# Local attention and two mixture layers on one core: where the softmax of batches 0 and 1 is normalised

## The chip, the cores and the metric

The kernel runs on one core of a Trainium2 chip. The metric is the device time of one execution in microseconds (us): a median of 918.62 us over 3 runs, from 918.5 to 919.01. One further execution was profiled and took 924.32 us, of which 922.5 us are the span from its first to its last instruction. That is 5.70 us above the median, so differences worked out on the profile are applied to the median afterwards.

## The reference, cut to what matters

Attention comes first: 4 batches, 8 heads, 512 local and 32 global positions, head size 64. Local queries see a window of 32 positions to either side and the 32 global keys. Two feed-forward stages follow.

```python
def sm(s):
    s = s - np.max(s, axis=-1, keepdims=True)
    e = np.exp(s)
    return e / (np.sum(e, axis=-1, keepdims=True) + 1e-09)
...
s_l = np.concatenate([s_lg, s_ll], axis=-1)
a_l = sm(s_l)
out_l = np.matmul(a_l, np.concatenate([v_g, v_l], axis=2))
...
h = x @ w_in
g = np.maximum(h, 0.0) + alpha * np.minimum(h, 0.0)
return (g @ w_out)
```

The division by the row sum is linear: it can be done on the probabilities `P` before the product with `V`, or on the product afterwards, row by row. The second feed-forward stage routes every token to one of 8 experts; its choice of expert needs all tokens.

## The kernel before, in words

**Tiling of the attention.** `units` are 16 pairs of heads: units 0 to 3 are batch 0, units 4 to 7 batch 1, and so on. A unit is done in two steps, j = 0 and 1, of 256 query positions each, and a step has two blocks of 128 queries for each of its two heads. For each step the functions in `attention()` run in this order, each for a step later than the one before:

- `scores` (L355): TensorE multiplies queries with 224 keys (L369) into two PSUM banks `s`. VectorE adds the mask and finds the maximum (L375, four instructions), ScalarE takes the exponential and the row sum `sm` (L377, four).
- `norm` (L380): VectorE adds 1e-9 to four columns of sums (L383), takes the reciprocal (L384), and multiplies the four 128 x 224 blocks of `pr` by it (L388).
- `ptrans` (L390): TensorE turns the probabilities (L397), ScalarE copies them to SBUF (L399).
- `pv` (L401): TensorE multiplies with the values (L408, eight products, written in pairs to partitions 0-63 and 64-127, so the output has head dimensions on partitions and queries along the columns). ScalarE copies the result to `x` (L409).

Each pair of units also has a global part: `gscores` (L420 to L426), `gnorm` (L430 to L432), `gtrans` (L439 to L446) and `gpv` (L457), whose result VectorE copies to `x` (L460).

**The first stage.** While `alone[0]` is true, only attention and the decoding of weights run. It goes on until batch 0 is complete. PSUM has 2 + 2 banks for `s`, 2 for `t`, and 2 with the tag `y`, which `o`, `gs`, `gt` and `go` share (`bank`, L317).

**The second stage.** Attention of batches 1 to 3 is then traced in turn with the first half of the first feed-forward layer: `gemm` (L174) works on chunks of 272 tokens, two chunks to a batch, with matmuls at L166 and L199. Its first matmul needs the split of chunk 0 (`splitx`, a copy on ScalarE and a subtraction on VectorE, both L67/L68), and so all of batch 0's columns up to 272. Four PSUM banks with the tag `a` serve the attention here.

**Decoding.** The weights come as 64-bit floats, read as pairs of integers. `decode` (L72) takes an absolute value on ScalarE (L77) and four passes on VectorE (L78, L80, L81, L82); `split` then copies on ScalarE (L67) and subtracts on GpSimd or VectorE (L68). There are 16 parts of 128 x 512 for the first half of the layer. The second half's 16 parts are decoded after the attention, in the memory that it leaves.

**What sets the order.** Up to the second half of that layer the order on each engine is not the order of the text: a planner in the tile framework goes over the traced instructions with its own estimates of time, and places what is ready by its estimate, earlier text first. Each engine then runs its list strictly in order. From the routing on, TensorE's order is written out by hand. Waits between engines are put in by the framework from the tiles that instructions read and write.

The functions that the change touches, and those that call them:

Of the kernel before, what the change touches and what calls it, by code (L numbers as in the profile page):

```python
# [9 lines left out]
F32 = mybir.dt.float32  # L10
# [5 lines left out]
OP = mybir.AluOpType  # L16
# [9 lines left out]
def tile_attention_moe_moe(ctx: ExitStack, tc: tile.TileContext, qkw, vw,  # L26
                           w_in, w_out, alpha, w_gate, w1, w2, out):
    nc = tc.nc
    V, A, P, T = nc.vector, nc.scalar, nc.gpsimd, nc.tensor
    B, H, S, D, SG = BHSDG  # L30
# [27 lines left out]
    ident = cp.tile([128, 128], F32, name="ident")  # L58
# [244 lines left out]
    with ExitStack() as at:  # L303
# [3 lines left out]
        tp = at.enter_context(tc.tile_pool(name="tp", bufs=2, side="right"))  # L307
# [9 lines left out]
        def bank(shape, name):  # L317
            pool, tag = pY, "y"
            if not alone[0]:
                pool, tag = pA[0], "a"  # L320
            elif name == "s":
                pool, tag = ((pS, "s"), (pS, "s"), (pH, "h1"), (pH, "h1"))[turn[0] % 4]
                turn[0] += 1
            elif name == "t":
                pool, tag = pX, "x"
            return pool.tile(shape, F32, name=name, tag=tag)

        units = [(b, hp) for b in range(B) for hp in range(H // 2)]
        NU = len(units)
        U = [dict() for _ in units]  # L330
        G = [dict() for _ in range(NU // 2)]
        KO = S + NB * KW

        def load(u):
            d = U[u]
            qk = ld.tile([128, KO + 2 * SG], F32, name="qk")
            cut_ = S + 2 * KW if u == 0 else 0
            if cut_:
                nc.sync.dma_start(out=qk[:, :cut_], in_=qkw[u, :, :cut_])
            nc.sync.dma_start(out=qk[:, cut_:], in_=qkw[u, :, cut_:])  # L340
            d["q"] = qk[:, :S]
            d["k"] = qk[:, S:KO].rearrange("p (i w) -> p i w", w=KW)
            d["g"] = qk[:, KO:]

        def load_v(u):
            d = U[u]
            vv = ld.tile([128, 2, NB, 2 * D], F32, name="vv", bufs=4)
            nc.sync.dma_start(out=vv.rearrange("p a i d -> p (a i d)"), in_=vw[u])
            d["va"], d["vb"] = vv[:, 0], vv[:96, 1]

        def heads(u):
            for h in range(2):
                yield h, slice(h * D, (h + 1) * D)

        def scores(u, j):  # L355
            d = U[u]
            if j == 0:
# [22 lines left out]
        def norm(u, j):  # L380
            d = U[u]
            sm = d["sm"][:, :, 2 * j:2 * j + 2]
            V.tensor_scalar(sm, sm, 1e-9, None, op0=OP.add)  # L383
            V.reciprocal(sm, sm)  # L384
            for ii in range(2):
                i = 2 * j + ii
                for h in range(2):
                    V.tensor_scalar(d["pr"][:, h, i], d["pr"][:, h, i], d["sm"][:, h, i:i + 1], None, op0=OP.mult)  # L388

        def ptrans(u, j, half):  # L390
            d = U[u]
            n = 96 if half else 128
            t = bank([n, 2, 2, 128], "t")
            for ii in range(2):
                for h in range(2):
                    p = d["pr"][:, h, 2 * j + ii]
                    T.transpose(t[:, ii, h], p[:, 128:KW] if half else p[:, 0:128], ident)  # L397
            d["t", j, half] = tp.tile([n, 2, 2, 128], F32, name="pt", tag="bt" if half else "at")
            A.copy(d["t", j, half], t)  # L399

        def pv(u, j):  # L401
            d = U[u]
            o = bank([128, 2, 128], "o")
            for ii in range(2):
                i = 2 * j + ii
                for half, v in enumerate(("va", "vb")):
                    for h, c in heads(u):
                        T.matmul(o[c, ii], d[v][:, i, c], d["t", j, half][:, ii, h], start=half == 0, stop=half == 1)  # L408
            A.copy(d["x"][:, SG + 256 * j:SG + 256 * j + 256], o.rearrange("p i t -> p (i t)"))  # L409

        def gscores(p, part):
            d = G[p]
# [59 lines left out]
        def attention():  # L472
# [7 lines left out]

            for n in range(2 * NU + 2):
                u, j = divmod(n, 2)
                if u < NU:
                    if j == 0 and u + 2 < NU:
                        load(u + 2)
                        load_v(u + 2)
                    scores(u, j)
                    yield 1.0
                if 1 <= n <= 2 * NU:
                    a_ = divmod(n - 1, 2)  # L490
# [6 lines left out]
                if n >= 2:  # L497
# [3 lines left out]
                    if v % 2 and j2:  # L501
                        gout(v // 2)
                        yield 0.1
                if u < NU and u % 2 == 0 and j:
                    p = u // 2
# [24 lines left out]
        while done[0] < UPB - 1:  # L530
            next(att)
            n += 1
            if n >= 6 and n % 6 == 0 and len(parts) > KD:
                f, i = parts.pop(0)
# [10 lines left out]
        c = 0  # L545
        g = None
        going = True
        while going:
# [6 lines left out]
            if spent["a"] <= spent["g"] * ratio or g is None:  # L555
                x = next(att, None)
# [4 lines left out]
            else:  # L561
                x = next(g, None)
# [3 lines left out]
                else:  # L566
                    spent["g"] += x
                    if parts:
                        f, i = parts.pop(0)
# [5 lines left out]
    with tc.tile_pool(name="dc2", bufs=1, side="right") as dc, tc.tile_pool(name="pW", bufs=2, space=PSUM) as pW:  # L575
# [3 lines left out]
        while c < NCH:  # L579
# [4 lines left out]
            while next(g, None) is not None:  # L584
                n += 1
                if n % 3 == 0 and parts:
                    f, i = parts.pop(0)
# [12 lines left out]
    with ExitStack() as mo:  # L600
# [44 lines left out]
        late = rc_.tile([128, 128], BF, name="late")  # L645
# [39 lines left out]
        for i, n in enumerate(TH + [1]):  # L685
            t = spot(n).bitcast(I32) if i else rc_.tile([128, n], I32, name="jt0")
# [571 lines left out]
```

## Time and profile before

| | |
|---|---|
| median of 3 runs | 918.62 us |
| profiled execution | 924.32 us, span 922.5 us |
| TensorE matmul busy | 854.1 us (93%) |
| VectorE busy | 561.1 us (61%) |
| ScalarE busy | 405.2 us (44%) |
| GpSimd busy | 402.1 us (44%) |
| mean granted TensorE clock | 0.966 of full speed |

PE is TensorE's matmuls, PEld its weight loads, DVE VectorE, ACT ScalarE, POOL GpSimd, SP the queue that issues most transfers. Times are from the span's start. A busy share over the span mixes stages with different limits, so each stage is read by itself. An f32 matmul is carried out as two recorded instructions, so the eight products of one `pv` appear as 16. Matmuls overlap, so a group's length contains the latency of its last one; what a group costs its engine is read from its start to the start of the next.

### The profile page before, as it was taken

What the parts mean: (1) busy time and instruction counts of PE and PEld (TensorE: products, weight loads), DVE (VectorE), ACT (ScalarE), POOL (GpSimd) and SP (SyncE); (2) the same over time, 40 slices, a digit from 0 to 9 for tenths busy, and PEclk for the clock granted to TensorE, in tenths of its full rate; (3) what the DMA queues carried; (4) which work ended last, traced back from release to release, by engine and by line L of the source; (5) the groups of instructions that cost most, each with busy time, mean ns of one, the idle gap of its engine ahead of it and who ended that gap; (6) DMA issues with size and microseconds to landing.
All of it is one profiled execution on the core that took longest, in us unless ns stands there. A gap on an engine that the chain in (4) does not pass through costs nothing.

```text
span 922.5 us, 18674 instructions
## 1 busy us (share of the span) xinstructions
PE 854.1 (93%) x7142; PEld 781.4 (85%) x7142; DVE 561.1 (61%) x1815; ACT 405.2 (44%) x945; POOL 402.1 (44%) x335
## 2 busy tenths in 40 slices
PE   6869999999998799999999897999699998899996
PEld 4648898888888799999998897999498998799995
DVE  6999665556549963266567767778266766631120
ACT  5866655455534542234332423331334534444431
POOL 2224211111115642176566515232467777777721
PEclk8988999999999999999999998999799999999998
DMA  8574323422136412032210224332445555455510
GB/s 305 178 251 159 123 74 115 118 72 88 37 129 178 146 49 73 23 100 83 65 49 1 74 72 157 98 100 87 125 141 162 162 161 174 151 164 181 168 40 35
DMA packets 50273, 107.66 MB, mean 117 GB/s; under 512 B 6728, under 2 KB 23112, under 8 KB 50184
## 3 DMA queue, kind: packets, MB, share of 16 engines
q1 hardware_dynamic: 47288, 97.56, 33.8%
q0 software_dynamic: 2896, 8.92, 2.7%
q8 instruction: 56, 0.92, 0.4%
q14 instruction: 33, 0.27, 0.1%
HBM read 88.63 MB, written 17.83 MB: 115 GB/s over the span
## 4 chain that ended last, share of the span: by engine, by line
PE 29%; DMA 10%; POOL 8%; issue 6%; DVE 3%; ACT 3%; POOLq 0%; SPq 0%; ACTq 0%
PE h L1103 10%; PE h L166 9%; DMA raw<-in_moe_w_dram 9%; POOL m L68 6%; PE h L979 2%; PE lp L238 2%; ACT m L67 2%; PE h L995 1%; POOL xg L930 1%; DVE gr L68 1%; PE yt L227 1%; PE y L199 1%; PE pc L819 1%; POOL out_dram L1029 0%; DMA x2d<-yr 0%
## 5 line engine op out<-in xcount | busy, mean ns | idle before, releaser
L68 POOL TENSOR_TENSOR m<-raw,m 128x1024 fp32r<-128x1024 f32 x64 | 152.6, 2390 | 58.3 <-ACT m L67 57.8
L166 PE MATMUL h<-xh,win 128*128 128x272 f32 x768 | 168.9, 300 | 7.5 <-ACT xh L67 3.7
L166 PEld LDWEIGHTS h<-xh,win 128*128 128x128 f32 x768 | 129.1, 192 | 15.4 <-DVE g L185 4.5
L68 POOL TENSOR_TENSOR glo<-g,ghi 128x272 fp32r<-128x272 f32 x64 | 57.6, 902 | 192.7 <-ACT ghi L67 190.6
L1103 PE MATMUL h<-gr,wout 128*128 128x272 f32 x768 | 115.1, 302 | 0.3 <-DVE gr L68 0.3
L166 PE MATMUL h<-xl,win 128*128 128x272 f32 x384 | 113.1, 295 | 1.7 <-DVE xl L68 1.7
L199 PE MATMUL y<-ghi,wout 128*128 128x272 f32 x512 | 111.8, 298 | 3.1 <-ACT ghi L67 3.0
L979 PE MATMUL h<-xsh,m 128*128 128x272 f32 x512 | 109.5, 303 | 5.2 <-ACT xsh L67 5.2
L171 DVE TENSOR_SCALAR nm<-h,al 128x272 f32<-128x272 f32 x128 | 63.4, 496 | 82.8 <-PE h L166 82.1
L1103 PEld LDWEIGHTS h<-gr,wout 128*128 128x128 f32 x768 | 103.0, 195 | 7.6 <-issue 6.6
L995 PE MATMUL h<-hh,m 128*128 128x272 f32 x512 | 103.4, 294 | 0.0
L67 ACT CAST m<-raw 128x1024 fp32r<-128x1024 f32 x64 | 66.8, 1047 | 79.8 <-DMA raw<-in_moe_w_dram 79.6
L979 PEld LDWEIGHTS h<-xsh,m 128*128 128x128 f32 x512 | 85.0, 195 | 6.5 <-ACT xsh L67 6.2
L199 PEld LDWEIGHTS y<-ghi,wout 128*128 128x128 f32 x512 | 84.0, 189 | 7.3 <-ACT ghi L67 3.9
L995 PEld LDWEIGHTS h<-hh,m 128*128 128x128 f32 x512 | 81.3, 189 | 0.9 <-issue 0.5
L199 PE MATMUL y<-glo,wout 128*128 128x272 f32 x256 | 75.3, 298 | 3.0 <-POOL glo L68 3.0
L979 PE MATMUL h<-xsl,m 128*128 128x272 f32 x256 | 76.8, 300 | 0.0
L166 PEld LDWEIGHTS h<-xl,win 128*128 128x128 f32 x384 | 74.2, 193 | 2.7 <-DVE xl L68 2.4
L995 PE MATMUL h<-hl,m 128*128 128x272 f32 x256 | 75.6, 295 | 0.1
L377 ACT ACTIVATE pr<-sc,mx 128x224 f32<-128x224 f32 x128 | 60.5, 475 | 25.4 <-DVE mx L375 25.3
L68 POOL TENSOR_TENSOR l<-gb,h 128x272 fp32r<-128x272 f32 x62 | 54.5, 893 | 22.9 <-ACT h L67 20.7
L375 DVE CUSTOM_DVE_ANT_0 sc<-s,mask 128x224 f32<-128x224 f32 x128 | 43.3, 383 | 31.4 <-PE s L369 31.4
(233 smaller groups left out, 1725.9 us busy)
## 6 DMA issues: line engine op xcount, KB each, us to landing
raw<-in_moe_w_dram SPq DMA_DIRECT2D x64, 512.0 KB, 3.6
qk<-in_qk_dram SPq DMA_DIRECT2D x15, 736.0 KB, 4.2
vv<-in_v_dram SPq DMA_DIRECT2D x16, 512.0 KB, 5.2
raw<-in_moe_w_in_dram SPq DMA_DIRECT2D x16, 512.0 KB, 5.5
raw<-in_moe_w_out_dram SPq DMA_DIRECT2D x16, 512.0 KB, 3.9
xs<-xb SPq DMA_DIRECT2D x16, 272.0 KB, 5.0
xpart<-xd SPq DMA_DIRECT2D x32, 136.0 KB, 1.8
xb<-xs SPq DMA_DIRECT2D x8, 544.0 KB, 4.3
```

What stands on the lines that cost most here:

```text
L67: A.copy(hi, src)
L68: (lo_eng or V).tensor_tensor(lo, src, hi.bitcast(F32), op=OP.subtract)
L166: T.matmul(ps, wi[:, w, k, fs], x[:, k], start=i == 0, stop=i == 3 * KD - 1)
L171: V.tensor_scalar(nm, ps, 0.0, al[:, hf * KH + f:hf * KH + f + 1], op0=OP.min, op1=OP.mult)
L199: T.matmul(ps, wo[:, w, f, ds_], x[:, f], start=i == 0, stop=i == 3 * KH - 1)
L227: T.transpose(t[:, k * 128:(k + 1) * 128], tail["x"][:, k] if q == 2 else xo[:, k, a:b], ident)
L238: T.matmul(lp, w, x, start=first and i == 0, stop=last and i == 1)
L375: V.tensor_tensor_reduce(out=sc, in0=s[h][:, ii], in1=m, scale=-D ** -0.5, scalar=BIG, op0=OP.add, op1=OP.min, accum_out=d["mx"][:, h, i:i ...
L377: A.activation(out=d["pr"][:, h, i], in_=sc, func=AF.Exp, bias=d["mx"][:, h, i:i + 1], scale=-1.0, accum_out=d["sm"][:, h, i:i + 1])
L979: T.matmul(ps, d["w1"][:, w, kk, fs], x[:, kk], start=i == 0, stop=i == 3 * KD - 1)
L995: T.matmul(ps, d["w2"][:, w, f, ms], x[:, f], start=i == 0, stop=i == 3 * K3 - 1)
L1103: T.matmul(ps[j], wo[:, w, f, ds_], x, start=f == 0 and a == 0, stop=f == KH - 1 and a == 2)
```

## The change

In batches 0 and 1 `norm` stops after the reciprocal: `pr` keeps the exponentials. In `pv` the PSUM tile doubles to two halves. TensorE first writes the reciprocals into the second half: the weights are one column of `sm`, repeated 64 times, the moving operand is the identity, so all 64 output partitions hold the row of 128 reciprocals. ScalarE copies that half to a new SBUF tile `rs`. The products with the values go to the first half as before, and VectorE multiplies the two into `x`, where ScalarE had copied. Batches 2 and 3 and the global rows are as before.

```diff
+        NBO = 2
...
             V.reciprocal(sm, sm)
+            if units[u][0] < NBO:
+                return
             for ii in range(2):
...
-            o = bank([128, 2, 128], "o")
+            late = units[u][0] < NBO
+            ot = bank([128, 2, 2, 128] if late else [128, 1, 2, 128], "o")
+            o = ot[:, 0]
+            if late:
+                for ii in range(2):
+                    for h, c in heads(u):
+                        T.matmul(ot[c, 1, ii], d["sm"][:, h, 2 * j + ii:2 * j + ii + 1].to_broadcast([128, D]), ident, start=True, stop=True)
+                rs = tp.tile([128, 2, 128], F32, name="rs")
+                A.copy(rs, ot[:, 1])
...
-            A.copy(d["x"][:, SG + 256 * j:SG + 256 * j + 256], o.rearrange("p i t -> p (i t)"))
+            x = d["x"][:, SG + 256 * j:SG + 256 * j + 256].rearrange("p (i t) -> p i t", i=2)
+            if late:
+                V.tensor_tensor(x, o, rs, op=OP.mult)
+            else:
+                A.copy(x, o)
```

## Rows read from the trace of the kernel before

**Rows 1.** The page's second part: busy tenths of each engine and TensorE's granted clock in 40 slices of 23 us.

```profile
PE   6869999999998799999999897999699998899996
...
DVE  6999665556549963266567767778266766631120
ACT  5866655455534542234332423331334534444431
...
PEclk8988999999999999999999998999799999999998
```

**Rows 2.** Busy time of each engine by stretch (the view by windows): stretch, its length, then PE, PEld, DVE, ACT and POOL busy with the number of instructions, the granted clock, the share of the DMA engines and GB/s.

```profile
6.00:16.00 10.00, 6.94 (x43) 4.23 (x40) 8.11 (x43) 5.75 (x21) 0.00 (x0) 1.00 1.02 400
16.00:40.00 24.00, 23.39 (x192) 16.76 (x192) 23.46 (x92) 22.21 (x72) 4.30 (x4) 0.79 0.58 174
40.00:52.00 12.00, 8.40 (x63) 5.97 (x63) 12.00 (x47) 10.09 (x30) 3.14 (x3) 0.79 0.98 333
52.00:66.00 14.00, 8.02 (x101) 6.25 (x100) 13.66 (x22) 8.16 (x15) 5.26 (x5) 0.94 0.60 172
66.00:76.00 10.00, 8.22 (x49) 6.79 (x49) 9.90 (x26) 6.55 (x18) 3.28 (x3) 0.66 0.73 254
76.00:92.00 16.00, 15.62 (x110) 13.05 (x109) 16.00 (x42) 8.77 (x23) 7.46 (x7) 1.00 0.40 129
92.00:140.00 48.00, 48.00 (x481) 42.88 (x481) 29.91 (x117) 28.17 (x86) 10.12 (x11) 1.00 0.31 99
140.00:266.00 126.00, 126.00 (x1197) 110.23 (x1193) 70.13 (x273) 67.16 (x202) 15.19 (x18) 1.00 0.26 81
266.00:322.00 56.00, 47.42 (x357) 44.59 (x356) 51.70 (x83) 26.64 (x52) 31.41 (x27) 1.00 0.57 178
```

**Rows 3.** The timeline at the end of the first stage, all engines: start, length, engine, line, operation, and in brackets the idle time before it with what ended it.

```profile
57.29 1.36 PE L457 MATMUL go<-gt,vv 128*64 128x32 f32 x40 [0.32 <-DVE gt L440]
...
58.66 1.73 DVE L81 SCALAR_TENSOR_TENSOR mag<-raw,mag 128x512 int32<-128x512 int32 x1
...
61.95 1.74 DVE L81 SCALAR_TENSOR_TENSOR mag<-raw,mag 128x512 int32<-128x512 int32 x1
63.73 0.69 DVE L82 SCALAR_TENSOR_TENSOR mag<-raw,mag 128x512 int32<-128x512 int32 x1
64.33 0.22 DVE L460 COPY xb<-go 128x64 f32<-128x64 f32 x1
...
64.98 1.09 ACT L67 CAST xh<-xb 128x1088 fp32r<-128x1088 f32 x1
...
66.12 0.52 PE L166 MATMUL h<-xh,win 128*128 128x272 f32 x2 [3.75 <-ACT xh L67]
```

**Rows 4.** VectorE's costliest groups from 0 to 66 us (the view by lines): count, busy, mean of one in ns, idle time before.

```profile
L375 DVE CUSTOM_DVE_ANT_0 sc<-s,mask 128x224 f32<-128x224 f32 x40 | 13.8, 379 | 6.3 <-PE s L369 6.3
L388 DVE TENSOR_SCALAR pr<-pr,sm 128x224 f32<-128x224 f32 x40 | 13.7, 400 | 0.0
L81 DVE SCALAR_TENSOR_TENSOR mag<-raw,mag 128x512 int32<-128x512 int32 x11 | 10.6, 962 | 0.2
```

**Rows 5.** What TensorE waited for from 0 to 66 us (the view of waits): total, times, longest.

```profile
PE o L408 <- DVE gmx L422: 3.2, 2, 2.4
PE s L369 <- DVE mx L375: 3.1, 1, 3.1
PE t L397 <- ACT pt L399: 1.0, 2, 0.6
PE gt L445 <- DVE gsc L432: 0.8, 1, 0.8
PE o L408 <- ACT xb L409: 0.7, 1, 0.7
...
PE go L457 <- DVE gt L440: 0.3, 1, 0.3
```

**Rows 6.** TensorE's timeline around one `pv` of the second stage, and ScalarE's copy of another.

```profile
112.21 0.41 PE L199 MATMUL y<-ghi,wout 128*128 128x272 f32 x2
112.56 1.10 PE L408 MATMUL o<-pt,vv 128*64 128x128 f32 x16
113.59 0.40 PE L199 MATMUL y<-glo,wout 128*128 128x272 f32 x1
...
115.60 0.29 PE L199 MATMUL y<-glo,wout 128*128 128x272 f32 x1
115.73 0.41 PE L199 MATMUL y<-ghi,wout 128*128 128x272 f32 x2
...
104.26 1.08 PE L408 MATMUL o<-pt,vv 128*64 128x128 f32 x16
105.39 0.37 ACT L409 COPY xb<-o 128x256 f32<-128x256 f32 x1 [1.95 <-PE o L408]
```

**Rows 7.** TensorE's `pv` instructions from 0 to 66 us (by lines), and those from 66 to 140 us with duration min/median/max in ns (the view of one line).

```profile
L408 PE MATMUL o<-pt,vv 128*64 128x128 f32 (+1 forms) x128 | 11.3, 322 | 4.4 <-DVE gmx L422 3.2 <-ACT xb L409 0.7 <-ACT gt L446 0.6
...
L408 PE MATMUL o<-pt,vv x128: 269/272/325, 75.0 to 137.5; 128*64 128x128 f32 x64, 96*64 96x128 f32 x64
```

**Rows 8.** Durations: a VectorE instruction with one PSUM and one SBUF operand (66 to 140 us), ScalarE's eight copies of `o` (0 to 66 us), and all multiplications of `pr` (min/median/max in ns).

```profile
L185 DVE SCALAR_TENSOR_TENSOR g<-h,nm 128x272 f32<-128x272 f32 x14 | 6.1, 435 | 0.7
...
L409 ACT COPY xb<-o 128x256 f32<-128x256 f32 x8 | 2.9, 365 | 0.0
...
L388 DVE TENSOR_SCALAR pr<-pr,sm x128: 319/331/1404, 9.3 to 254.7; 128x224 f32<-128x224 f32 x128
```

**Rows 9.** By windows, as rows 2, around TensorE's early change of clock.

```profile
12.00:16.00 4.00, 0.94 (x9) 0.59 (x6) 3.61 (x19) 1.94 (x7) 0.00 (x0) 1.00 1.02 407
16.00:20.00 4.00, 3.39 (x16) 2.10 (x15) 3.46 (x13) 3.35 (x10) 0.00 (x0) 0.53 0.85 179
20.00:24.00 4.00, 4.00 (x26) 2.98 (x24) 4.00 (x16) 3.69 (x13) 1.45 (x1) 0.50 0.92 300
24.00:28.00 4.00, 4.00 (x28) 2.55 (x26) 4.00 (x17) 4.00 (x16) 0.00 (x0) 0.69 0.46 177
28.00:32.00 4.00, 4.00 (x32) 2.97 (x28) 4.00 (x18) 4.00 (x11) 1.31 (x1) 1.00 0.38 125
```

**Rows 10.** VectorE's waits for TensorE's `gpv` from 92 to 266 us.

```profile
DVE xb L460 <- PE go L457: 5.0, 3, 3.7
```

## The prediction, on record before the changed kernel ran

> **What bounds the kernel now.** I read the busy tenths by slice first. TensorE is full from about 70 us to the end of the attention and has holes before; VectorE is full from the second slice to the fourth [rows 1]. So the attention lies in two stages with different limits, and the change touches both: by TensorE's `pv` instructions, 128 before 66 us and 128 from 75.0 to 137.5 us, 16 to a step, batch 0's eight steps lie in the first stage and batch 1's eight in the second [rows 7].
>
> The view by windows says which engine is short. From 16 to 66 us VectorE is busy 49.1 of 50 us, while ScalarE has 9.5 and TensorE 10.2 us to spare. From 66 to 92 VectorE is still full, but TensorE is busy 23.8 of 26, and from 92 to 266 us it is busy without a break, with VectorE at 57% [rows 2]. From 66 us on, then, TensorE sets the pace, and what VectorE does less of there buys nothing.
>
> The timeline at the border shows how the first stage ends: `gpv` ends at 58.65, yet VectorE copies it at 64.33, because decoding of weights stands in front in its list; the split of the first chunk and the first matmul of the feed-forward layer at 66.12 follow directly [rows 3]. VectorE's list is the chain that ends the stage.
>
> After the attention nothing changes. Decoding the second half of the weights begins when the attention gives its memory back and keeps VectorE busy 51.7 of 56 us [rows 2], so that stage starts earlier or later with the attention's end, and I carry the difference to the end of the kernel one to one.
>
> **The change part by part.** *Removed in the first stage.* All 40 multiplications of `pr` that the first stage holds, ten steps of units 0 to 4, which all fall under the change, stand in front of the 64.33 copy; together they keep VectorE 13.7 us [rows 4]. One takes 319 to 1404 ns [rows 8]; the group's total has the stretched ones in it.
>
> *Added there on VectorE.* Eight multiplications of 128 x 256 with one operand in PSUM. The nearest row is 435 ns for 272 columns [rows 8]; I take 0.43 us, so 3.4 us. VectorE's list gets 13.7 - 3.4 = 10.3 us shorter.
>
> *ScalarE.* One copy of 256 columns from PSUM goes (365 ns) and one of the same size comes: nothing, by count [rows 8]. The copy moves ahead of the products, so it can wait for TensorE while exponentials are queued behind it; I cost that with the rival on handoffs.
>
> *Added on TensorE.* Four f32 products per step, with 128 columns moving and 64 weight columns in pairs, half of what `pv` does. `pv` takes from 112.56 to 113.59, 1.03 us, among the feed-forward matmuls [rows 6], so half is 0.515 us. From below, nothing excludes that they fill a hole: 0 in the first stage. From above: where they stand alone, a change of kind is paid twice more. Feed-forward matmuls start 0.13 us apart (115.60, 115.73), so the second of the pair at 112.21 started at 112.34 and the next was due at 112.47; `pv` came 0.1 us late [rows 6]. That makes 0.61 us at most.
> The Trainium skill, "TensorEngine Tiling (Array Packing)", Key Properties under Tiling Modes, says that changing the tiling mode drains the engine, and the new products differ in mode from the feed-forward matmuls. That is a price for every separate block; the trace has it at about 0.1 us, and the sum by the rule would be that upper end.
>
> *What the first stage gains.* With VectorE 10.3 us shorter, its copy could stand at 54.0. TensorE is next. Its waits for VectorE from 5 to 66 us are 3.1 + 3.2 + 0.8 + 0.3 = 7.4 us [rows 5]. If all went, and the eight new blocks came in at 0.515 us, twice as much for two of them between 16 and 27 us, where the granted clock is at its lower level [rows 9] (8 x 0.515 + 2 x 0.515 = 5.2 us at most; the last one isn't needed by chunk 0, so 4.6), `gpv` would end at 58.65 - 7.4 + 4.6 = 55.9. So the matmul at 66.12 could come at most 8.5 us earlier. The lower end is 0: the planner can put more decoding in front, as it does now. Not every wait for VectorE will go, since decoding moves into the holes; I take two thirds, 5.7 us.
>
> *What the second stage loses.* Batch 1's eight blocks on a full engine: 8 x 0.515 = 4.1 to 8 x 0.61 = 4.9 us, taken as 4.5. The norms that go there were beside TensorE: no gain. From below: TensorE's holes between 66 and 92 us are 2.2 us [rows 2], and blocks that fall into them all would leave 1.9; less than nothing is excluded, since the products are added to an engine that is full from 92 us on.
>
> *The sum.* 5.7 - 4.5 = 1.2 us gained: 923.1 for the profiled execution, 917.4 for the median. Two large terms nearly cancel, so the sign is not safe. About 0.2% (1.84 us) is what a measurement of this kernel can tell from no change.
>
> **The rivals.** *The handoff inside one bank.* The reciprocals and the output share one PSUM tile. If the framework holds the products back until ScalarE has read `rs`, TensorE goes to ScalarE and back in every step. Priced by rows: the last product's own 0.27 us [rows 7], then ScalarE's copy, which today starts within 0.05 us of the products' end and takes 0.37 [rows 6], and about 0.1 back: 0.8 us if nothing else is placed between. Eight times that in the first stage is 6.4 us on the engine that I found to be next; half of it, because scores and transposes of other steps can stand between, is 3.2. Then the first stage gains 5.7 - 3.2 = 2.5 and the sum is +2.0: 920.6. It decides on the slower side once more than 1.2 us of the 6.4 are not covered. For it: TensorE already waits 0.7 us for such a copy to free a bank, and 3.2 us for the shared `y` banks, which are held longer now [rows 5]. Against it: the planner knows the wait and has other work for TensorE from 16 to 40 us.
> The Trainium skill, "PSUM — Partial Sum Buffer", section on PSUM bank collisions, says that two engines on the same bank and quadrant at once are an error and that software has to order them. By that rule the wait is real and the question is only what covers it; no run here shows it yet.
>
> *The end of the first stage stays where decoding puts it.* VectorE's freed time is filled with more parts of the weights, which stand before the 64.33 copy again. A part is four passes; L81 alone took 1.73 us twice there [rows 3], so two more parts eat half of the 10.3 us or more. A multiplication that waits for TensorE can hold the list too: one wait for `gpv` was 3.7 us [rows 10]. The gain falls to 2 us and the sum is +2.5: 921.1. For it: that is what the rows show today. Against it: those parts are then missing later, but TensorE is full there, so they bring nothing back.
>
> *The clock stays up.* After 3.1 us idle TensorE's granted clock falls at 16 us to its lower level of 1.2 GHz and is back by 28 [rows 5, 9]. That idle time ends with VectorE's L375, behind four multiplications which go. Shorter, it might leave the clock at 2.4 GHz; the 11 us of nearly full work until 27 would take half, and about 3 us of it could reach the end of the stage, where ScalarE, with 9.5 us to spare [rows 2], sets a limit of its own. The sum is -4.2: 914.4. For it: the engine before was at the higher level up to the gap. Against it: ScalarE waits for transfers in the same place.
>
> *The change does not do what it says* in one sense: that norms vanish from VectorE but the stage was held by TensorE's own work all along. From 16 to 40 us TensorE is busy 23.4 of 24 [rows 2]. Then the blocks come on top in both stages, 4.6 + 4.5 us less a few waits of the 7.4: about +4, 922.6.
>
> **How the numbers follow.** The two terms nearly cancel as worked out (from +0.4 to -2.9 us): 0.44, of which 0.20 lie beyond -1.84 and 0.24 within 0.2%. Clock stays up, or VectorE's relief reaches further: 0.20, all faster. Handoff: 0.16, of which 0.03 within 0.2%. The end stays with decoding: 0.12, of which 0.01 within. TensorE's own work: 0.08, slower. That is faster 0.40, same 0.28, slower 0.32. The forecast is that of the first case, 917.4, whose own range is 915.7 to 919.0. The range of 8 in 10 takes in -5 us at one end and +4 at the other: 913.6 to 922.4.
>
> **What would show it.** Right: VectorE's L388 falls from 128 to 64 instructions; the first feed-forward matmul comes at 59 to 62 us instead of 66.12; from there to the end of the attention the stretch is 4 to 5 us longer than 200; from 266 us on lengths are the same. The handoff would show as waits of TensorE's `o` for ScalarE's `rs`, the clock as a level near 1.0 from 16 to 28 us, decoding as a late L460 with `gpv` long done. I'd be wrong if TensorE's blocks in the second stage cost clearly more or less than 0.5 to 0.6 us, or if the stage after the attention doesn't move along with its start.

## The result, and the profile after

The changed kernel took 928.07 us (median of 4 runs, 926.8 to 929.41), the kernel before 918.82 beside it (918.5 to 919.74). These two medians are 9.25 us apart; the ratio on record is 1.0083, 95% interval 1.0053 to 1.0112: slower by 0.8%. In the later series, with 9 to 25 executions each, the kernel before has medians of 920.22 to 921.25. The forecast was 917.4, its range 913.6 to 922.4; the time lies outside. The profiled execution took 928.45 us with a span of 926.7.

Three points of time tell where it went. The first feed-forward matmul came at 71.2 us (before: 66.1), the attention's last transfer `xs` was issued at 274.3 (266.5), the last matmul `h<-xh,win` of the first layer at 502.7 (495.1). So the attention ends 7.8 us later, and the first layer behind it moves along. From the attention's end to the end of the span the profiles of this study have 645 to 656 us (656.0 before, 652.4 after), and these lengths don't go with the number of new products. Profiles are therefore compared up to the attention's end. There is one profile of each kernel, though, and executions of one kernel differ by several us (the kernel before from 917.12 to 925.28 over all series), so a difference of a few us between two profiles can be one of executions.

The page's busy tenths and the granted clock after, in the slices of [rows 1]:

```profile
PE   7889999999998899999999898999699999899996
...
DVE  4989546465638984355656867777266766541120
ACT  5776555555534452233332333331244544444431
...
PEclk8879999999999899999999998999799999999999
```

The slices are too wide for this change: TensorE looks fuller than before, and the time is longer. By windows (as rows 2), the kernel after:

```profile
6.00:16.00 10.00, 9.97 (x62) 5.98 (x58) 5.16 (x29) 5.88 (x21) 0.00 (x0) 1.00 1.00 396
16.00:40.00 24.00, 20.20 (x149) 13.69 (x147) 21.53 (x72) 18.65 (x53) 6.45 (x5) 0.72 0.61 188
40.00:52.00 12.00, 7.84 (x74) 5.03 (x72) 11.79 (x32) 9.32 (x26) 3.71 (x4) 0.85 0.78 249
52.00:66.00 14.00, 13.12 (x135) 10.13 (x135) 9.58 (x36) 9.78 (x31) 2.01 (x2) 0.76 0.67 232
66.00:76.00 10.00, 7.67 (x72) 5.87 (x73) 9.90 (x22) 8.58 (x21) 4.32 (x3) 1.00 0.76 260
92.00:140.00 48.00, 48.00 (x440) 40.91 (x440) 24.65 (x98) 26.55 (x79) 7.87 (x9) 1.00 0.25 78
```

VectorE got its relief: its 40 multiplications of `pr` up to 66 us [rows 4] have gone, and six short ones have come there (view by lines, 0 to 66 us):

```profile
L376 DVE CUSTOM_DVE_ANT_0 sc<-s,mask 128x224 f32<-128x224 f32 x40 | 14.0, 382 | 7.2 <-PE s L370 6.5 <-ACT pr L378 0.6
L81 DVE SCALAR_TENSOR_TENSOR mag<-raw,mag 128x512 int32<-128x512 int32 x10 | 9.9, 986 | 0.1
...
L422 DVE TENSOR_TENSOR xb<-o,rs 128x256 f32<-128x256 f32 x6 | 2.5, 419 | 0.0
```

It is busy 5.16 us instead of 8.11 in the first stretch, 9.58 instead of 13.66 in the fourth [rows 2]. TensorE used it: it is busy 9.97 of 10 us in the first stretch (6.94 before) and 13.12 of 14 in the fourth (8.02). But from 16 to 40 us, where it had been full, it now idles 3.8 us, with ScalarE and VectorE idle beside it, and its granted clock, which is at one of its two levels, 1.2 and 2.4 GHz, has a lower mean there than before: 0.72 against 0.79, and 0.76 against 0.94 from 52 to 66 us. From 66 to 76 us it is the other way round, 1.00 against 0.66.

What TensorE waited for from 0 to 66 us (as rows 5):

```profile
...
PE t L400 <- ACT pt L402: 3.1, 3, 1.9
PE o L419 <- ACT rs L414: 1.8, 2, 1.3
PE gs L435 <- DVE gmx L437: 1.5, 1, 1.5
PE go L472 <- DVE gt L455: 0.9, 1, 0.9
PE o L412 <- DVE xb L422: 0.7, 1, 0.7
...
```

The long waits for VectorE are gone, 3.2 and 3.1 us [rows 5]. Waits for ScalarE have come: 3.1 us for its copies of `pt` (1.0 before) and 1.8 for the new `rs`.

What ends the first stage has changed with that. The first chunk needs the seventh `pv` of batch 0. Before, it started at 55.87 us, and VectorE's copy of `go` came 5.7 us behind `gpv`'s end [rows 3]. After, that copy comes 0.4 us behind `gpv`'s end, but TensorE reaches the seventh `pv` only at 66.62, together with the eighth, and VectorE's new multiplications and the split follow it (timelines, before and then after):

```profile
55.87 1.10 PE L408 MATMUL o<-pt,vv 128*64 128x128 f32 x16 [0.57 <-ACT gt L446]
```

```profile
63.41 1.31 PE L472 MATMUL go<-gt,vv 128*64 128x32 f32 x40
...
65.09 0.19 DVE L475 COPY xb<-go 128x64 f32<-128x64 f32 x1
...
66.62 1.98 PE L419 MATMUL o<-pt,vv 128*64 128x128 f32 x32
...
68.59 0.41 DVE L422 TENSOR_TENSOR xb<-o,rs 128x256 f32<-128x256 f32 x1
...
69.72 1.10 ACT L67 CAST xh<-xb 128x1088 fp32r<-128x1088 f32 x1
```

The end of the attention is read from TensorE's own account up to it. One window from 0 to the end of the attention, before and then after:

```profile
0.00:266.50 266.50, 246.82 (x2232) 208.25 (x2233) 183.27 (x656) 158.53 (x464) 52.66 (x66) 0.96 0.41 134
```

```profile
0.00:274.30 274.30, 258.58 (x2360) 213.79 (x2361) 172.45 (x608) 160.37 (x464) 53.48 (x66) 0.96 0.40 130
```

The same 2232 matmul instructions stand before the end of the attention in both, feed-forward ones included, and 128 new ones. TensorE is busy 11.8 us longer and idle 15.7 instead of 19.7 us; 11.8 - 4.0 = 7.8 us is the whole delay. Busy and idle time add up to the end in any kernel, so this says where the time went and not yet what took it. VectorE's 10.8 us less don't appear in it. The new instructions have this group (view by lines, 0 to 274.3 us), with 12.1 us of their own:

```profile
L412 PE MATMUL o<-ident,sm 128*64 128x128 f32 x128 | 12.1, 305 | 1.0 <-DVE xb L422 0.7 <-ACT gt L461 0.2
```

### The profile page after: what moved, and what is told of

Same layout as the page of the kernel before. It is cut to its first block, busy times and chain, and to the rows that moved or that the text cites. A ratio compares the mean times of both kernels' runs of the same rounds, so it can differ in the third digit from the quotient of the medians.

```text
span 926.7 us, 18880 instructions
## 1 busy us (share of the span) xinstructions
PE 864.5 (93%) x7270; PEld 786.3 (85%) x7270; DVE 550.1 (59%) x1767; ACT 407.0 (44%) x945; POOL 403.4 (44%) x335
## 4 chain that ended last, share of the span: by engine, by line
PE 32%; DMA 7%; POOL 6%; issue 5%; DVE 4%; ACT 3%; POOLq 0%; SPq 0%; ACTq 0%
PE h L1118 10%; PE h L166 9%; DMA raw<-in_moe_w_dram 6%; POOL m L68 4%; PE h L1010 3%; PE h L994 3%; PE lp L238 2%; ACT m L67 2%; POOL xg L945 1%; DVE gr L68 1%; PE yt L227 1%; PE y L199 1%; PE pc L834 1%; POOL out_dram L1044 1%; DMA x2d<-yr 0%
## 5 line engine op out<-in xcount | busy, mean ns | idle before, releaser
L166 PE MATMUL h<-xh,win 128*128 128x272 f32 x768 | 166.4, 296 | 3.2 <-DVE g L185 2.5
L199 PE MATMUL y<-ghi,wout 128*128 128x272 f32 x512 | 115.1, 301 | 1.4 <-ACT ghi L67 1.3
```

The source lines that it names most:

```text
L166: T.matmul(ps, wi[:, w, k, fs], x[:, k], start=i == 0, stop=i == 3 * KD - 1)
L199: T.matmul(ps, wo[:, w, f, ds_], x[:, f], start=i == 0, stop=i == 3 * KH - 1)
```

## The experiments

The runs came in five series, and theories fell on the way: first the lifetime of the sums and the place of the decoding, then the handoff between engines. The account above was the last and is tested at the end, with a mixed outcome. All runs in one table, from profiles up to the attention's end (us). "Low" is the part of TensorE's busy time that the lower clock took: busy time times one minus the granted clock, added up over windows of 1 us. "Ratio" is to the kernel before in the same series, with its 95% interval.

| run | first feed-forward matmul | attention's end | TensorE busy | low | idle | median | ratio |
|---|---|---|---|---|---|---|---|
| before | 66.1 | 266.5 | 246.8 | 10.7 | 19.7 | 918.82 | 1 |
| after | 71.2 | 274.3 | 258.6 | 10.7 | 15.7 | 928.07 | 1.0083 [1.0053, 1.0112] |
| e1_no_norm | 68.6 | 266.8 | 248.9 | 14.1 | 17.9 | 919.21 | 0.9992 [0.9971, 1.0013] |
| e2_adds_only | 74.8 | 283.4 | 266.8 | 20.6 | 16.6 | 930.32 | 1.0106 [1.0075, 1.0137] |
| e3_batch0_only | 71.7 | 270.8 | 253.2 | 10.8 | 17.6 | 920.44 | 0.9998 [0.998, 1.0017] |
| e4_batch1_only | 66.2 | 280.6 | 259.7 | 15.6 | 20.9 | 928.18 | 1.0082 [1.0055, 1.011] |
| e5_own_bank | 76.7 | 282.1 | 259.9 | 16.5 | 22.2 | 932.16 | 1.0111 [1.0075, 1.0147] |
| e6_no_norm_held | 60.7 | 264.2 | 250.3 | 9.5 | 13.9 | 916.63 | 0.9957 [0.993, 0.9983] |
| e7_before_held | 56.6 | 258.9 | 242.4 | 2.8 | 16.5 | 909.22 | 0.9872 [0.9838, 0.9905] |
| e8_after_held | 63.3 | 268.3 | 253.6 | 4.6 | 14.7 | 921.43 | 1.0006 [0.9987, 1.0024] |
| e9_after_sums4 | 71.0 | 274.4 | 259.0 | 10.9 | 15.4 | 923.51 | 1.0031 [1.0008, 1.0054] |
| e10_batch1_sums4 | 65.8 | 275.3 | 253.6 | 10.2 | 21.7 | 928.22 | 1.0094 [1.006, 1.0127] |
| e11_after_held_sums4 | 65.7 | 273.7 | 256.4 | 4.7 | 17.3 | 923.42 | 1.0037 [1.001, 1.0065] |
| e12_batch0_held_sums4 | 65.1 | 267.2 | 248.1 | 3.1 | 19.1 | 918.92 | 0.9983 [0.9966, 1.0001] |
| e13_early_held | 63.2 | 270.8 | 256.3 | 8.3 | 14.5 | 919.54 | 0.9987 [0.9972, 1.0002] |
| e14_dvecopy_held_sm4 | 63.1 | 272.7 | 254.3 | 6.1 | 18.4 | 925.67 | 1.0068 [1.0047, 1.0089] |
| e15_batch0_early_held | 58.9 | 266.6 | 248.8 | 1.7 | 17.8 | 919.59 | 0.9994 [0.9978, 1.0009] |
| e16_before_held_sums4 | 56.8 | 259.2 | 242.6 | 3.1 | 16.6 | 907.58 | 0.9873 [0.984, 0.9906] |
| e17_batches_2_3 | 67.7 | 285.8 | 265.8 | 10.3 | 20.0 | 933.31 | 1.0134 [1.0113, 1.0154] |
| e18_products_twice | 72.3 | 282.3 | 262.5 | 9.2 | 19.8 | 934.44 | 1.0146 [1.012, 1.0172] |

The profiled executions of e2, e4 and e5 took 8.3, 5.9 and 5.8 us more than the medians of their runs, and their stretches behind the attention are ordinary (652 to 654 us). Their attention's ends in the table are therefore likely some us late for these kernels.

**The parts alone.** The removal without the additions, e1_no_norm, which leaves batches 0 and 1 without their normalisation (diffs are against the changed kernel):

```diff
-            late = units[u][0] < NBO
+            late = False
```

> Batches 0 and 1 are left without normalisation: the multiplications of P go and nothing takes their place. Theory A (VectorE's freed time is given to weight decoding, whose ScalarE and VectorE instructions then stand in front of the exponentials): the removal alone brings nothing in the first stage, first feed-forward matmul at 65 us or later, total 917 to 925 us. Rival B (the added products, copies and handoffs on TensorE and ScalarE cost the 9 us): the removal alone gains what I forecast for it, matmul at 58 to 62 us, total 911 to 914 us.

The additions without the removal, e2_adds_only, which divides twice:

```diff
-            if units[u][0] < NBO:
-                return
```

> All additions of the change with the multiplications of P kept (rows of batches 0 and 1 are normalised twice). Theory A: VectorE stays as full as before, so no decoding is moved forward; what is left is the added work, 3 to 5 us in the second stage and 1 to 3 in the first: 922 to 926 us. Rival B: at least the changed kernel's 928 us, 928 to 934.

The removal alone is worth nothing: 0.9992, with 1 inside its interval, and the attention ends at 266.8 instead of 266.5. The additions alone cost 1.06%, about what the whole change costs. The first result was expected by theory A and the second by rival B; neither theory had both. In the kernel without multiplications TensorE's groups from 0 to 266.8 us show where the relief went: its transposes now wait 8.2 us for ScalarE, where the kernel before had 1.0 [rows 5].

```profile
L400 PE MATMUL t<-ident,pr 128*128 128x128 f32 (+1 forms) x256 | 42.4, 293 | 8.4 <-ACT pt L402 8.2
```

In the table this kernel's idle time is 1.8 us less than before, and the lower clock takes 3.4 us more.

Batch 0 alone, e3_batch0_only:

```diff
-        NBO = 2
+        NBO = 1
```

> The change in batch 0 alone. Both theories leave the first stage's loss of about 5 us in place, and the second stage's loss of 2.7 to 4.5 us goes: 923 to 925 us. If the loss of the first stage came from unit 4's steps, which are traced there and belong to batch 1, it would be near 919.

Batch 1 alone, e4_batch1_only, in `norm` and in `pv`:

```diff
-            if units[u][0] < NBO:
+            if units[u][0] == 1:
...
-            late = units[u][0] < NBO
+            late = units[u][0] == 1
```

> The change in batch 1 alone: eight blocks of products of 0.515 to 0.61 us on a full TensorE, 4.1 to 4.9 us, and two of the ten steps in the first stage lose their multiplications: 921.5 to 924 us. If below 920, the second stage has room for the blocks and the whole loss is the first stage's.

Batch 0's part is free by the median, 0.9998, and batch 1's part costs what both cost, 1.0082. Both medians lie outside what was expected (920.44 against 923 to 925, 928.18 against 921.5 to 924). The profiled executions (922.99 and 934.07 us) are the longest of their runs. In them each part adds busy time (6.4 and 12.9 us) and neither takes off much idle time (2.1 less, 1.2 more). From the first feed-forward matmul to the attention's end it is 203.1 us after and 199.1 with batch 0 alone: batch 1's eight blocks cost 4.0 us there, by this pair of profiles. The ratios make it twice that (1.0083 against 0.9998, 7.8 us), and no run settles which is nearer.

**The handoff in one bank.** The products of the sums get a PSUM tile of their own:

```diff
-            ot = bank([128, 2, 2, 128] if late else [128, 1, 2, 128], "o")
-            o = ot[:, 0]
+            o = bank([128, 2, 128], "o")
...
+                rt_ = bank([128, 2, 128], "t")
...
-                A.copy(rs, ot[:, 1])
+                A.copy(rs, rt_)
```

> The reciprocals go to a PSUM tile of their own instead of the second half of the output's, so the products need not wait for ScalarE's copy. Rival B (the handoff inside one bank): most of the 1.8 us of TensorE's waits for that copy in the first stage go and 3 us or more of the loss: 922 to 925 us. Theory A (decoding moved forward, and TensorE's own added work in the second stage): no gain, 926 to 930 us.

It got slower still, 1.0111, and its median lies above both ranges: `o` no longer waits for `rs`, but the two banks of `t` are now shared, and the transposes wait 5.8 us for them. This run doesn't settle the handoff, since it moved the wait.

**Decoding held behind the exponentials.** In the changed kernel decoding stands between the exponentials. ScalarE's timeline, after:

```profile
35.60 0.48 ACT L378 ACTIVATE pr<-sc,mx 128x224 f32<-128x224 f32 x1
...
36.07 0.68 ACT L77 ACTIVATE mag<-raw 128x512 f32<-128x512 f32 x1
...
40.32 0.69 ACT L77 ACTIVATE mag<-raw 128x512 f32<-128x512 f32 x1 [1.41 <-POOL win L68]
...
44.35 0.69 ACT L77 ACTIVATE mag<-raw 128x512 f32<-128x512 f32 x1 [1.19 <-POOL win L68]
...
46.41 0.48 ACT L378 ACTIVATE pr<-sc,mx 128x224 f32<-128x224 f32 x1
```

No exponential starts for 10.8 us, and ScalarE waits for other engines' decoding in between. So each part of the decoding was queued behind the latest exponential traced before it (in the second stage behind the first stage's last one), in the kernel without normalisation, in the one before, and in the one after:

```diff
-                    A.activation(out=d["pr"][:, h, i], in_=sc, func=AF.Exp, bias=d["mx"][:, h, i:i + 1], scale=-1.0,
+                    lastexp[0] = A.activation(out=d["pr"][:, h, i], in_=sc, func=AF.Exp, bias=d["mx"][:, h, i:i + 1], scale=-1.0,
...
-                f(dc, 0, i)
+                with tc.issue_after(lastexp[0].ins):
+                    f(dc, 0, i)
```

> As the kernel without normalisation in batches 0 and 1, but ScalarE's instructions of the decoding are queued behind the latest exponential traced (those traced after the first stage behind its last one). Theory A (VectorE's freed time is spent on decoding that stands in front of the exponentials): now the removal shows: the first feed-forward matmul comes at 58 to 63 us instead of 68.6. The end falls by 2 to 6 us (913 to 917), unless the decoding then comes late for the second stage. If the exponentials are not held up by decoding, the matmul stays at 66 to 69 us.

> The kernel before with the same hold on the decoding. Theory A: VectorE is full with its multiplications there, decoding is already late, so the hold changes little: 917 to 921 us, first matmul at 63 to 67 us. If the hold helps here as much as without the multiplications, it is not the freed time that matters.

> The changed kernel with the same hold. Theory A: the first stage's loss of 5 us goes, first matmul at 62 to 66 us, and 4 to 5 us of added products in the second stage stay: 921 to 925 us. Rival B (added work and handoffs make the first stage's loss): 926 us or more, first matmul near 71 us.

It helps all three, and the kernel before most: 909.22, a ratio of 0.9872, where 917 to 921 had been expected. That beats both kernels. Its attention ends 7.6 us earlier, 7.9 of them from the lower clock (10.7 to 2.8) and 3.2 from idle time, with 3.5 given back. So the place of the decoding is a loss of its own and not what the change added: held, the change still costs 9.4 us up to the attention's end (268.3 against 258.9) and 12.2 by the medians. The larger part of that comes with the removal alone, which has no product at all: 5.3 us, and 7.4 by the medians, with 6.7 us of waits for ScalarE's `pt` (e6_no_norm_held, 0 to 66 us).

```profile
PE t L402 <- ACT pt L404: 6.7, 4, 3.7
```

The additions on top of the removal cost 4.1 us held, 4.8 by the medians; without the hold they cost 7.5 us, and 8.4 by the ratios (after against e1).

**The lifetime of the sums.** `sm` has two buffers and is now read until `pv`, so the exponentials of a unit must wait for products of the unit two before. With four buffers:

```diff
-                d["sm"] = pp.tile([128, 2, NB], F32, name="sm")
+                d["sm"] = pp.tile([128, 2, NB], F32, name="sm", bufs=4)
```

The same for batch 1 alone, and with decoding held for both batches and for batch 0:

> The changed kernel with four buffers for the row sums instead of two. Theory C (the new products read the row sums a step later, so with two buffers the exponentials of unit u+2 wait for unit u's products; decoding then takes their place in ScalarE's list): the 11 us hole in the exponentials between 35.6 and 46.4 us goes, the first feed-forward matmul comes at 63 to 68 us instead of 71.2, total 921 to 925 us. If the hole comes from the planner's filling freed time (theory A) it stays, 926 to 930 us.

> The change in batch 1 alone, with four buffers for the row sums. Theory C: the 8 us shrink to the price of the added products on a full TensorE, 4 to 5 us: 922 to 926 us, and TensorE is not at its lower clock between 78 and 91 us. If the second stage's loss is only the products and the handoffs, it stays at 926 to 930.

> The changed kernel with the decoding held behind the exponentials and four buffers for the row sums. Theory C: the first stage ends as early as in the kernel before with the hold (56.6 us) or up to 3 us later, and what is left against that kernel's 909 is the second stage's 4 to 5 us: 912 to 916 us. Without theory C: as with two buffers, 919 to 923.

> Batch 0 alone, with the hold and four buffers: a version that could beat both kernels. If VectorE's relief is worth something in the first stage once nothing is in its way, this is below the 909 us of the kernel before with the hold: 904 to 908. If the relief is worth nothing, 908 to 914.

The hole among the exponentials closes: the last one of the first stage, the fortieth, starts at 51.48 us instead of 64.17 (e9_after_sums4).

```profile
51.48 0.48 ACT L378 ACTIVATE pr<-sc,mx 128x224 f32<-128x224 f32 x1
```

So the exponentials of that hole were not ready: in the main they waited for the sums' buffers, and the decoding filled the time. Yet the first feed-forward matmul comes at 71.0 us, where 63 to 68 had been expected, and the attention ends at 274.4, as after. The median is 4.6 us lower (the intervals of the two ratios touch, and the profile up to the attention's end has no gain that would answer to it), and with batch 1 alone or with decoding held there is none. With decoding held the medians lie above what theory C expected: 923.42 against 912 to 916, and for batch 0 alone 918.92, above both its ranges (904 to 914). The wait for the buffers was real, and taking it away didn't bring the end forward. What is left with decoding held looks like the handoff (TensorE's waits, e11_after_held_sums4):

```profile
PE o L421 <- ACT rs L416: 5.5, 3, 3.4
```

**The handoff once more, and a control.** Products and copy one step earlier, in `t`'s banks, so that nothing but VectorE's last multiplication needs the copy (e13_early_held, and e15_batch0_early_held with `NBO = 1`), in `ptrans`:

```diff
+            if half and units[u][0] < NBO:
+                r = bank([128, 2, 128], "t")
...
+                d["rs", j] = tp.tile([128, 2, 128], F32, name="rs")
+                A.copy(d["rs", j], r)
```

The copy made by VectorE, with four buffers (e14_dvecopy_held_sm4):

```diff
-                A.copy(rs, ot[:, 1])
+                V.tensor_copy(rs, ot[:, 1])
```

And as a control the kernel before with four buffers. All four have decoding held.

> The change in both batches, decoding held, and the products of the sums with ScalarE's copy moved one step earlier, right behind the transposes of P, in a PSUM tile of their own; nothing waits for the copy but VectorE's multiplication two steps on. Theory H (handoff): TensorE's waits of the attention products for the copy go (11.9 us for three in the run with four buffers, 3.5 in the held one), and the first feed-forward matmul comes at 57 to 60 us instead of 63.3 or 65.7; the median is 914 to 918 (921.4 less 3 to 7). Theory P (the order as such): it stays at 63 to 67 us and the median at 920 to 924.

> As the held kernel with four buffers for the sums, and the copy of the products made by VectorE instead of ScalarE. Theory H, in the form that ScalarE's list delays the copy behind conversions that wait for transfers: the waits of 5.5 us get short (under 2 us), the first feed-forward matmul comes at 58 to 62 us, the median at 916 to 920. If the handoff costs by the round trip itself, whoever copies: 63 to 66 us and 920 to 924.

> As the run with the early products, but the change for batch 0 alone, so no blocks of products in the second stage. Theory H: first feed-forward matmul at 57 to 60 us, second stage 4 us shorter than with both batches; median 910 to 914, that is like the kernel before with decoding held (909.2). Theory P: 63 to 67 us, median 916 to 920. Should the removal of the multiplications be worth what the prediction gave it, it would come clearly under 909.

> Control: the kernel before, decoding held, with four buffers for the row sums, which it doesn't need. If buffers and memory layout alone don't shift anything, the first feed-forward matmul comes at 56 to 58 us as before and the median is 907 to 911. If the planner's order is so easily disturbed that any edit costs several us (theory P), it comes at 60 us or later and the median is over 913.

The 11.9 us in the first of these expectations counts the idle time of TensorE's weight loads as well; its matmuls waited 5.5 us, as shown above. The early form has no wait of `o` for the copy any more (the transposes wait 3.9 us for it instead, in their banks), and its attention ends at 270.8, still 11.9 us behind the held kernel before. Its median, 919.54, is near theory P's range. VectorE's copy cut the wait from 5.5 to 3.5 us and gained no time (925.67, above both ranges). So no run took the handoff's waits away without bringing others. The run for batch 0 is the telling one: its first feed-forward matmul comes at 58.9 us, 2.3 behind the held kernel before, and its attention ends 7.7 behind; its median, 919.59, is theory P's. The time of that first matmul, by which the prediction and most of my theories went, doesn't set the end. The control is as fast as without the buffers (907.58, 0.9873), so this edit by itself doesn't upset the planner's order.

In place of the waits, the account of the table: TensorE's busy time without its "low" part is 235 to 241 us in the five kernels with no products (before, e1, e6, e7, e16), 242 to 247 in the five with one batch, 243 to 252 in the eight with batches 0 and 1, each product computed once. By the means, 238.2, 244.4 and 247.8, that is 0.6 to 0.8 us a block over many forms of waits. Each group spreads by 5 to 8 us, so the means carry this and no single pair does.

**TensorE's own time.** The change in batches 2 and 3, where TensorE is full (e17_batches_2_3), in `norm` and in `pv`:

```diff
-            if units[u][0] < NBO:
+            if units[u][0] >= NBO:
...
-            late = units[u][0] < NBO
+            late = units[u][0] >= NBO
```

> The change made in batches 2 and 3 instead of 0 and 1: all sixteen blocks of products lie in the second stage, VectorE's multiplications go only there, and the first stage is that of the kernel before. If TensorE's own time until the end of the attention sets that end (theory O): the first feed-forward matmul stays at 65 to 68 us, the attention ends 16 x 0.68 = 10.9 us later than 266.5, at 276 to 279, idle time stays near 20 us, and the median is 10 to 12 above the kernel before, 929 to 932. If the price in a full TensorE is the 0.515 to 0.61 of the prediction: 8.2 to 9.8, so 927 to 930. If the loss of the change is one of the first stage (handoffs, order, lifetime of the sums), most of it goes away here, and the median lies under 926.

Every product computed twice into the same place (e18_products_twice):

```diff
                     for h, c in heads(u):
-                        T.matmul(ot[c, 1, ii], d["sm"][:, h, 2 * j + ii:2 * j + ii + 1].to_broadcast([128, D]), ident, start=True, stop=True)
+                        for _ in range(2):
+                            T.matmul(ot[c, 1, ii], d["sm"][:, h, 2 * j + ii:2 * j + ii + 1].to_broadcast([128, D]), ident, start=True, stop=True)
```

> The changed kernel with every product of the sums computed twice into the same place, which adds nothing but TensorE time: 128 more instructions, without another change of kind, so 8 x 0.065 = 0.52 us a block and 8 to 10 us in all (part of them at the lower clock). Theory O: the attention ends at 281 to 285 us instead of 274.3, and the median is 935 to 939. If waits of TensorE set the end and its own work fits into them, it rises by half of that or less: 928 to 933.

Sixteen blocks in the full stage made it slower than the change itself: 1.0134, 12.5 us, with the first feed-forward matmul at 67.7. The 64 multiplications that it takes from VectorE there bought nothing. Its attention ends at 285.8, later than the 276 to 279 expected, and its median lies above the 929 to 932: 13 more feed-forward matmuls stand before the end (1.7 us), and some 5 us of longer instructions in the profile stay unexplained. The median rules out that the loss belongs to the first stage alone, for which it should have come under 926. The doubled products end the attention 8.0 us later, inside what was expected of it; their group grew from 12.1 to 20.6 us:

```profile
L413 PE MATMUL o<-ident,sm 128*64 128x128 f32 x256 | 20.6, 300 | 2.8 <-DVE xb L423 2.2 <-DVE gt L456 0.6
```

Its median rose 6.4 us over that of the changed kernel, to 934.44, a little less than the 935 to 939 expected. The 8.0 us aren't all TensorE's work:

```profile
0.00:282.30 282.30, 262.52 (x2488) 222.12 (x2489) 171.79 (x608) 160.71 (x464) 52.34 (x66) 0.96 0.39 126
```

Against the changed kernel it is 3.9 us busier and 4.1 us longer idle, and TensorE's waits for `rs` rose to 4.0 us up to 66 us (1.8 after). So the agreement with the expected end is in part luck, and the run doesn't part the products from the handoff that follows them. What the runs show is that the additions cost the time and the removal wins none; that TensorE's own time is the larger part of it is argued from the account and the price of a block below.

## Why the prediction was wrong

**The step that failed is "What the first stage gains".** It was put at 5.7 us, from 0 to 8.5; the first feed-forward matmul came 5.1 us later. The step measured the gain at that matmul and at VectorE's late copy. But the attention's work that isn't done by then follows behind, mixed with a fixed number of feed-forward matmuls, so only TensorE's idle time and its time at the lower clock can be won. Up to the first feed-forward matmul the idle time fell from 17.6 to 14.2 us, by 3.4; a gain of 5.7 with 4.6 us of new blocks would have needed 10.3. The clock took 10.7 us there instead of 7.7, and the new products 6.9 us up to 66 us, not 4.6. What comes late there now is TensorE's seventh `pv` (66.62 against 55.87 us) and no longer VectorE's copy. By the medians the change in batch 0 alone wins nothing (0.9998).

**Why the waits did not become time.** The relief of VectorE was right: VectorE has 10.8 us less up to the attention's end, and a new multiplication takes 0.419 us, where I had taken 0.43. The waits for VectorE fell too. ScalarE, which I had written off with 9.5 us to spare, took their place: 8.2 us of TensorE's waits in the kernel with the removal alone. Spare time added up over 50 us doesn't mean that its list is ready when TensorE needs it.

**The second stage** was expected 4.5 us longer, at 0.515 to 0.61 us a block. One block among feed-forward matmuls, after:

```profile
97.34 0.29 PE L166 MATMUL h<-xh,win 128*128 128x272 f32 x1
97.56 0.66 PE L412 MATMUL o<-ident,sm 128*64 128x128 f32 x8
98.15 0.40 PE L166 MATMUL h<-xh,win 128*128 128x272 f32 x1
```

The next matmul was due 0.13 us behind 97.34 and comes at 98.15: 0.68 us a block, 5.4 for eight. By the same reading a `pv` costs 113.59 - 112.47 = 1.12 us [rows 6]. Half the instructions save 0.44 us, 0.055 each; 0.24 us is the fixed price of a separate block, which I had halved with the rest and put at 0.1 above it. The five blocks that stand alone among feed-forward matmuls after all cost 0.67 to 0.68 us; the doubled ones of e18 cost 1.16, which makes the fixed part 0.20. The stretch itself was only 2.7 us longer, since the clock, at 1.2 GHz for part of 66 to 76 us before [rows 2], stayed up there after: the lower clock took 3.0 us of this stretch before and nothing after, and without that it is 5.7 us longer. The pair with batch 0 alone says 4.0, the ratios 7.8. So this term was too small as well, by about 1 us by the blocks and 3 by the ratios.
The Trainium skill, "TensorEngine Tiling (Array Packing)", Key Properties under Tiling Modes, says that a change of tiling mode drains the engine. The trace agrees that a separate block has a price, 0.24 us where I had given it 0.1; no run here shows how much of it is the drain.

**The carry to the end** holds as far as it can be read: from the attention's end to the last `h<-xh,win` of the first layer it is 228.6 us before and 228.4 after. Behind that the profile after is 3.4 us shorter, while the medians are 9.25 us apart, more than the 7.8 at the attention's end; with one profile each this isn't explained.

**The rivals.** "TensorE's own work all along", at 0.08 and about +4 us, is the one that comes nearest; it was too small by the products' size and by the waits that it let go. The handoff is there (1.8 us of waits after), but moving it out of the way gained at most 2 us by the medians (921.43 held, 919.54 with the early form), and it came back as other waits, so its price stays open. Decoding in front of other work is real and costs the kernel before about 12 us by the medians, but the change didn't bring it. The clock did not stay up: 0.72 from 16 to 40 us, 0.79 before.

What stays open: why the removal, with decoding held, makes the end 5.3 us later and the median 7.4 us longer than without it (the lower clock has 6.7 us more there, behind waits for ScalarE), which the account by TensorE's products doesn't cover; how the cost of the additions parts into products and handoff; and what makes the part behind the attention differ by up to 11 us between the profiles.

## What to carry to other kernels

Count, for the engine that ends the stage, its instructions up to a point behind all the work that the change touches, and ask whether their number changes; a first instruction that starts earlier is no gain if the same work stands before that point. Work moved to the engine that is full is paid at once, and the relief of the other only shows where the full engine was waiting for it and no third engine is next. Where executions of one kernel differ by several us, hold a reading of two profiles against the medians. For small blocks of another kind take the price from the gap between the neighbours' starts, and split it into a fixed part and one per instruction before halving it.

## What was not expected of the hardware

A block of eight f32 instructions between other matmuls cost 0.68 us and one of sixteen 1.12 to 1.16, so 0.20 to 0.24 us doesn't go down with the size. And the order of one engine's list reached TensorE's clock: holding decoding behind the exponentials left TensorE's work as it was and brought the mean granted clock from 16 to 40 us from 0.79 to 0.88 (the window below, e7_before_held, as in rows 2), so that the time given to the lower level up to the attention's end fell from 10.7 to 2.8 us.

```profile
16.00:40.00 24.00, 23.09 (x199) 16.68 (x201) 22.70 (x95) 21.34 (x70) 4.39 (x3) 0.88 0.61 188
```
